# An attention forward with recurrent memory, one core: V's heads in four column tiles, V's tail rows as a pass of their own, two buffers for scaled O

## The chip, the cores and the metric

One core of a Trainium2 chip runs one program: forward and backward of a transformer block. The metric is device time in microseconds of one execution, the median over several runs. TensorE (PE) multiplies, and loads stationary operands (PEld); VectorE (DVE) and ScalarE (ACT) move results from PSUM to SBUF and do elementwise work; GpSimd (POOL) copies within SBUF and issues some DMAs; SyncE (SP) issues the others.

## The reference

Attention goes over 64 segments of 32 rows. Each segment puts 8 memory rows ahead of its own 32, attends over these 40 rows in 32 heads of 128 columns, and the first 8 rows of its output are the memory of the next segment. Around it stand a layer norm with modulation, a gated unit, and the gradients of all of it.

```python
def _A_ref(x, mem0, Wq, Wk, Wv, Wo, seg_len):
    ...
    for s in range(n_seg):
        xs = x[:, s * seg_len:(s + 1) * seg_len, :].copy()
        h = jnp.concatenate([mem, xs], axis=1)
        q = jnp.einsum('btd,dhe->bhte', h, Wq)
        k = jnp.einsum('btd,dhe->bhte', h, Wk)
        v = jnp.einsum('btd,dhe->bhte', h, Wv)
        scores = jnp.einsum('bhqe,bhke->bhqk', q, k) * scale
        scores = jnp.where(mask[None, None], scores, -1000000000.0)
        p = _softmax(scores, axis=-1)
        o = jnp.einsum('bhqk,bhke->bhqe', p, v)
        o = jnp.einsum('bhte,hed->btd', o, Wo)
        mem = o[:, :M, :].copy()
        outs.append(o[:, M:, :])
    return jnp.concatenate(outs, axis=1)

x = A_x
...
h = _layernorm(x, axis=-1) * (1 + ca) + sa
x = x + ga * _A_ref(h, A_mem0, A_Wq, A_Wk, A_Wv, A_Wo, A_seg_len)
h = _layernorm(x, axis=-1) * (1 + cb) + sb
x = x + gb * _B_ref(h, B_w_gate, B_w_up, B_w_down)
```

## The kernel before

`phase2` is the forward of the attention; the phases behind it (gated unit, its gradients, gradients of the attention, gradients of the weights) are touched only where the last segment prepares them.

A segment's 40 rows are kept as 32 rows (the memory and the first 24 of its own rows; these depend on the segment before) and 8 tail rows (its last 8; these depend on the input alone). Four segments make a tile of 128 input rows; s4 is a segment's place in its tile. The 4 x 8 tail rows of a tile (`hb`) are projected together, ahead of their segments. Heads are packed three to a group: group g holds heads 3g, 3g+1 and 3g+2 in its rows 0-31, 32-63 and 64-95, and their tail rows in 96-119. There are 11 groups of 128 columns; the last has two heads.

All projections have 32 stationary columns, so four matmuls run side by side in the four column tiles of PE, each with its own 32 rows of the PSUM tile. K and Q use all four: three for heads 0 to 23, and the fourth for heads 24 to 31.

V is computed in three chunks (`v_chunk`, line 701 on; `v_mm`, line 675) of 4, 4 and 3 groups, with one column tile for each of the three heads of a group; each goes over the four parts c of the 512 inputs. During chunks 0 and 1 the fourth column tile computes V of the tail rows of the next tile (`VTAILS`): a third of the heads per segment and the last groups in the fourth segment. `RBv` holds these rows, 32 hl + 8 s4 for head hl of a group; `v_tails` copies them with three DMAs of POOL's queue into rows 96 to 119 of the segment's `Vst`. For tile 0 `v_first` does the same work in three tiles alone.

The order is written out by hand: the program order of each engine is pinned (`self.pin(i0)`), so no engine runs anything ahead. In a segment, PE runs: K and Q (line 257), chunk 0 of V, the turns of K and Q to columns (line 880), chunk 1, the scores of 11 groups onto a mask already in PSUM (line 890), chunk 2, the sums of exponentials of thirds 0 and 1 (line 896), the products with V of thirds 0 and 1 (line 916), sums and product of third 2, a fill that depends on s4 (0: a piece of the output product of tail rows, L215; 1: the turn of a layer-normed input tile, L422; 2 and 3: the turn of projected tail rows of K or Q, L638), the turns of scaled O (line 908 for third 0, line 950 for thirds 1 and 2), small turns for the output rows of earlier segments (L339), the output product (line 223), another fill, and the sum that gives the next memory.

ACT takes the exponentials (line 892) in three thirds of 4, 4 and 3 groups into `ET`, and scales the second third of O (line 937). DVE takes the reciprocals of the sums (line 901) and scales the first and last third (line 940). `Ost` holds scaled O; it has one buffer, and its store to `OSR` in DRAM is issued by SP (line 1069) behind the stores of K and Q and the DMA transposes of V and of the probabilities. POOL normalises the transposed probabilities of the segment before (line 1118), issues `v_tails`, and copies the tail columns of K and Q of the next segment. The PSUM pool of most of this has five buffers.

The last segments also prepare the first tile of the gated unit (`first_tile_steps`): vectors are broadcast from DRAM into buffers that are no longer in use, and x1, the block's input plus the gated attention output, is formed with its statistics.

Of the kernel before, what the change touches and what calls it, by code (L numbers as in the profile page):

```python
# [40 lines left out]
class K:  # L41
# [336 lines left out]
    def phase1_setup(self, ctx, psum_tile_fn):  # L378
# [56 lines left out]
        self.xh_tile = lambda: p1w.tile([128, D], F32, name="xh", bufs=1)[:]  # L435
        self.hx_tile = lambda: p1w.tile([128, DC, 128], BF16, name="hx", bufs=3)[:]
# [10 lines left out]
    def phase2(self):  # L447
# [12 lines left out]
        self.first_x1 = wq.tile([128, D], F32, name="x1_0")  # L460
        self.first_st = wq.tile([128, 12], F32, name="st_0")
        self.glu_tiles()
        with ExitStack() as ctx:
# [31 lines left out]
            Ost = ptiles("Ost", 1)[0]  # L495
# [3 lines left out]
            RBv = ptiles("RBv", 2)  # L499
# [120 lines left out]
            def b_pieces(t):  # L620
# [30 lines left out]
                return {(3, "f1"): [P("k", 0, 4, "dve")]}, {(1, "f1"): [P("k", 4, 4, "dve")], (1, "f2"): [P("q", 0, 2, "act")],  # L651
# [13 lines left out]
            VCH = ((0, 4), (4, 4), (8, 3))  # L665

            VTAILS = {(s4, k): ((s4,) + VCH[k] + (0,),) for s4 in range(3) for k in range(2)}
            VTAILS[3, 0] = ((0, 8, 3, 0), (1, 8, 1, 3))
            VTAILS[3, 1] = ((1, 9, 2, 0), (2, 8, 2, 2))

            def v_mm(ps, j, c, lhsT, hl, a, n, o=0):

                wc = Wv[:, c, :].rearrange("p (h e) -> p h e", e=E)
                n = min(n, (H - hl + 2) // 3 - a)
# [4 lines left out]
            def v_evac(eng, dst, ps, a, n):  # L679

                m = n if a + n < G else n - 1
                self.evac(eng, dst[0:96, a * E:(a + m) * E], ps[0:96, 0:m * E])
                if m < n:
                    self.evac(eng, dst[0:64, (a + m) * E:(a + n) * E], ps[0:64, m * E:n * E])

            def hb_rows(t):
                return lambda c: hxs[t][1][:, c, :, :].rearrange("p s q -> p (s q)")

            def v_first():

                for a, n in VCH:
                    ps = psp.tile([128, 512], F32, name="pass_ps", tag="p")
                    for c in range(DC):
                        for j in range(3):
                            v_mm(ps, j, c, hb_rows(0)(c), j, a, n)
                    v_evac("dve", RBv[0], ps, a, n)
# [25 lines left out]
            def first_tile_steps():  # L722
# [6 lines left out]
                bc5 = []  # L729
# [11 lines left out]

                def bc_3():
                    bc[3] = self.xh_tile()
                    bc_load(3, bc[3])
# [10 lines left out]
                def bc_5():  # L755
                    for i in range(2):
                        bc5.append(f32(self.hx_tile().rearrange("p c x -> p (c x)")))
                        bc_load(5, bc5[i], D // 2 * i, D // 2)

                def gates():  # L760
                    for i in range(2):
                        sl = slice(D // 2 * i, D // 2 * i + D // 2)
                        nc.vector.tensor_tensor(db[:, sl], dout[:, sl], bc5[i], op=ALU.mult)
# [1723 lines left out]
```

## Time and profile before

| what | us |
|---|---|
| median of 3 runs | 2979.73 |
| their range | 2972.82 to 2981.01 |
| the profiled execution | 2976.49 |
| its span | 2974.4 |
| PE busy in it | 2905.7 |
| granted clock in it, mean | 0.997 |

The 40 slices of the span, some 74 us each; the forward takes the first 13:

```
PE   6999999999998999999999999999999999999999
PEld 3666666666665544445677777777777754445545
DVE  5565666656655788733456666666566532850011
ACT  3666666666665544312355555555555520110011
POOL 2555545545545222221344444444444432762111
PEclk9999999999999999999999999999999999999999
DMA  9898888988899998899698999999999997876565
```

A digit is the busy share of a slice in tenths. Matmuls are pipelined and each is shown with its whole latency, so a full PE may still leave gaps between starts; what PE does is read from the starts of its instructions in order of time. A line number there is that of the instruction, or of a helper that many callers share; the tile's name tells which call it is.

### The profile page before, as it was taken

To read this page: it belongs to the slowest core of one execution; us is meant where nothing else is said; L and a number is where in the kernel's file an instruction comes from. 1 tells how busy PE (TensorE), PEld (TensorE's weight loads), DVE (VectorE), ACT (ScalarE), POOL (GpSimd) and SP (SyncE) were. 2 spreads that over 40 slices of the span, in tenths; PEclk is the share of its full clock that TensorE was granted. 3 is DMA by queue.
4 is the path that set the end of the run, shared out by engine and by line. 5 is a ranking of instruction groups with operands and counts; after the bars stand their busy time and mean duration, and the time that the engine had idled before them with its cause. 6 is when DMAs were issued, how large, how long until landed. Compare 5 with 4: busy or idle time off the path is not lost.

```text
span 2974.4 us, 105326 instructions
## 1 busy us (share of the span) xinstructions
PE 2905.7 (98%) x43742; PEld 1816.9 (61%) x43816; DVE 1620.3 (54%) x3683; ACT 1348.0 (45%) x3244; POOL 1233.2 (41%) x2486
## 2 busy tenths in 40 slices
PE   6999999999998999999999999999999999999999
PEld 3666666666665544445677777777777754445545
DVE  5565666656655788733456666666566532850011
ACT  3666666666665544312355555555555520110011
POOL 2555545545545222221344444444444432762111
PEclk9999999999999999999999999999999999999999
DMA  9888898988999899998699999999999997876565
GB/s 308 221 223 220 213 218 229 217 216 224 223 226 267 209 234 229 246 280 274 190 252 256 252 250 252 249 253 247 253 251 252 247 274 246 262 252 191 161 215 171
DMA packets 838066, 703.01 MB, mean 236 GB/s; under 512 B 537698, under 2 KB 710162, under 8 KB 836692
## 3 DMA queue, kind: packets, MB, share of 16 engines
q1 hardware_dynamic: 711972, 485.29, 66.3%
q0 software_dynamic: 54512, 148.63, 15.8%
q10 hardware_dynamic: 71104, 62.34, 6.5%
q8 instruction: 345, 5.65, 0.8%
q14 instruction: 133, 1.09, 0.1%
HBM read 294.99 MB, written 276.35 MB: 192 GB/s over the span
## 4 chain that ended last, share of the span: by engine, by line
PE 89%; DMA 5%; DVE 2%; issue 2%; ACT 1%; SPq 1%; POOL 1%; DVEq 0%; POOLq 0%; ACTq 0%
PE gps L2267 14%; PE pass_ps L257 14%; PE dh_ps L215 8%; PE g_ps L1890 5%; PE pass_ps L675 5%; PE gps5o L2282 4%; PE dhq_ps L223 4%; PE at_ps L223 4%; PE mm L1371 3%; PE gps L1550 3%; PE dh_tps L215 3%; PE turn_ps L880 2%; PE mm L1331 2%; PE mm L1346 2%; PE tps L1807 2%
## 5 line engine op out<-in xcount | busy, mean ns | idle before, releaser
L2267 PE MATMUL gps<-rows,hrows 128*128 128x512 bf16 (+2 forms) x2124 | 413.6, 355 | 1.9
L2267 PEld LDWEIGHTS <-hrows 128*128 128x128 bf16 x2160 | 211.1, 98 | 204.5 <-issue 0.9
L1118 POOL TENSOR_TENSOR Pst<-Pst,rden 120x1408 bf16<-120x1408 bf16 x63 | 159.7, 2535 | 315.1 <-issue 204.0
L63 DVE CAST ot<-gps 128x512 bf16<-128x512 f32 (+3 forms) x76 | 48.2, 634 | 310.8 <-PE gps L2267 229.2
L61 ACT ACTIVATE ot<-gps 128x512 bf16<-128x512 f32 (+3 forms) x75 | 41.2, 549 | 355.0 <-PE gps L2267 228.0
L1935 POOL COPY dOst<-RAd 96x512 bf16<-96x512 bf16 x128 | 75.1, 611 | 297.0 <-DVE RAd L63 297.0
L675 PE MATMUL pass_ps<-Wv,hT 128*32 128x512 bf16 (+2 forms) x2304 | 186.7, 357 | 0.0
L2271 POOL DMA_DIRECT2D out_dram<-ot x104 | 78.5, 755 | 257.6 <-DVE ot L63 133.4
L257 PEld LDWEIGHTS <-hT 128*32 128x32 bf16 x4096 | 117.0, 97 | 96.5 <-issue 6.2
L63 DVE CAST Vst<-pass_ps 96x512 bf16<-96x512 f32 x128 | 87.1, 681 | 106.5 <-ACT RBv L61 103.0
L215 PE MATMUL dh_ps<-WvT,dVT 128*32 128x512 bf16 x2048 | 133.4, 380 | 1.8 <-DVE RBd L63 0.2
L223 PE MATMUL at_ps<-Wo,OT 128*32 128x256 bf16 x4096 | 127.8, 276 | 1.2 <-ACT OT L61 1.0
L675 PE MATMUL pass_ps<-Wv,hb 128*32 128x512 bf16 (+2 forms) x636 | 126.5, 339 | 0.2 <-POOL hb L428 0.2
L257 PE MATMUL pass_ps<-Wk,hT 128*32 128x512 bf16 x2048 | 122.7, 380 | 2.1 <-POOL hT L561 1.1
L257 PE MATMUL pass_ps<-Wq,hT 128*32 128x512 bf16 x2048 | 124.1, 381 | 0.0
L257 PE MATMUL pass_ps<-WoT,dyT 128*32 128x256 bf16 (+1 forms) x3072 | 122.6, 308 | 0.9 <-ACT dyT L2016 0.9
L223 PE MATMUL dhq_ps<-WqT,dQT 128*32 128x256 bf16 x4096 | 122.9, 273 | 0.0
L215 PE MATMUL dh_ps<-WkT,dKT 128*32 128x512 bf16 x2048 | 122.3, 380 | 0.0
L2282 PE MATMUL gps5o<-WoT,rows 128*128 128x512 bf16 x549 | 120.4, 379 | 1.2 <-DMA rows<-OSR 0.6
L223 PEld LDWEIGHTS <-dQT 128*32 128x32 bf16 x4096 | 109.8, 97 | 15.7
L317 DVE TENSOR_TENSOR dST<-dh_ps,dST 128x512 bf16<-128x512 f32 x64 | 44.3, 692 | 130.0 <-ACT dST L316 130.0
L1877 DVE SCALAR_TENSOR_TENSOR dS<-dp_ps,Pst_l 128x480 bf16<-128x480 f32 (+1 forms) x192 | 106.3, 610 | 10.0 <-PE dp_ps L1875 4.1
(475 smaller groups left out, 7038.6 us busy)
## 6 DMA issues: line engine op xcount, KB each, us to landing
OSR<-Ost SPq DMA_DIRECT2D x64, 352.0 KB
OT<-OT SPq DMA_DIRECT2D x64, 352.0 KB
PS<-Pst SPq DMA_DIRECT2D x64, 352.0 KB
Pst_l<-PS SPq DMA_DIRECT2D x64, 352.0 KB
OT_l<-OT SPq DMA_DIRECT2D x64, 352.0 KB
DVR<-rows_x POOLq DMA_DIRECT2D x64, 352.0 KB, 6.3
DKR<-rows_x POOLq DMA_DIRECT2D x64, 352.0 KB, 6.1
DQR<-rows_x POOLq DMA_DIRECT2D x64, 352.0 KB, 3.2
```

Of the source, the lines that this page charges most:

```text
L63: return nc.vector.tensor_copy(out, in_)
L215: self.nc.tensor.matmul(ps[32 * j:32 * j + 32, :], lhsT=lhsT, rhs=w, start=(n < 4), stop=(n >= total - 4), tile_position=(0, 32 * j))
L223: nc.tensor.matmul(ps[32 * j:32 * j + 32, :], lhsT=x[k], rhs=w[k][:, 256 * d:256 * d + 256], start=(n == 0), stop=(n == total - 1), tile_p ...
L257: self.nc.tensor.matmul(ps[32 * j:32 * j + 32, :], lhsT=lhs(c), rhs=rhs, start=(c == 0), stop=(c == DC - 1), tile_position=(0, 32 * j))
L675: nc.tensor.matmul(ps[32 * j:32 * j + 32, o * E:(o + n) * E], lhsT=lhsT, rhs=wc[:, 3 * a + hl:3 * (a + n - 1) + hl + 1:3, :], start=(c == ...
L1118: nc.gpsimd.tensor_tensor(Pst[0:120, :, :], Pst[0:120, :, :], rden[:, :].unsqueeze(2).to_broadcast([120, G, 128]), op=ALU.mult)
L1371: nc.tensor.matmul(hp[:], lhsT=xT[:, fc, :], rhs=wT[:, fc, :], start=(n == 0), stop=(n == 2 * FC - 1))
L1550: nc.tensor.matmul(ps[:], lhsT=h2r[:, j, c * 128:(c + 1) * 128], rhs=xr[:, j, :], start=(j == 0), stop=(j == NT - 1))
L1877: nc.vector.scalar_tensor_tensor(out=part3(dS, pi)[:, :, 0:120], in0=ps[:, 0:n, 0:120], scalar=cfg.scale, in1=part3(Pst, pi)[:, :, 0:120], ...
L1890: nc.tensor.matmul(ps[:, j, 0:w], lhsT=lh[:, g * GW:(g + 1) * GW], rhs=rh[:, g * GW:g * GW + w], start=True, stop=True)
L2267: nc.tensor.matmul(ps[:, 0:ng * E], lhsT=hrows[:, tp_, c * 128:(c + 1) * 128], rhs=rows[:, tp_, 0:ng * E], start=(tp_ == 0), stop=(tp_ == ...
L2282: nc.tensor.matmul(pss[gg][:], lhsT=rows[:, t, gg * E:(gg + 1) * E], rhs=dyrows[:, t, :], start=(n == 0), stop=(n == NTP - 1))
```

## The change

V's heads are dealt out as K's and Q's are. The chunks have 3, 3 and 2 groups in the first three column tiles, which makes 8 groups; the fourth column tile computes the remaining groups 8 to 10: those of the first head in chunk 0 (three groups), of the second in chunk 1 (three), of the third in chunk 2 (two). DVE evacuates all chunks' 96 rows and the fourth tile's rows of chunks 0 and 1, and ACT the fourth tile's rows of chunk 2.

V of the tail rows becomes `v_tail`: a pass over two steps of 128 columns in four column tiles, four such passes per tile, evacuated by DVE, one in each segment, at a new place "gap" between the turns of O's first third and those of the others. For tile 0 two passes of four steps take the place of `v_first`. `RBv` now has the form of K's and Q's tail rows, and `v_tails` copies it with six DMAs instead of three.

`Ost` has two buffers, and 120 of its 128 rows are stored. The fill that followed the product of O's last third is issued ahead of that third's sums and product.

x1 of the first tile lies in the memory of Wk instead of a tile of its own, so its last step comes behind K's last pass; two broadcast vectors are loaded in halves into other buffers; and the input buffers of the gated unit's tiles are dealt out in another order.

```diff
-            Ost = ptiles("Ost", 1)[0]
+            Osts = ptiles("Ost", 2)
...
-            RBv = ptiles("RBv", 2)
+            RBv = ptiles("RBv", 2, w=9 * 128)
...
-                return {(3, "f1"): [P("k", 0, 4, "dve")]}, {(1, "f1"): [P("k", 4, 4, "dve")], (1, "f2"): [P("q", 0, 2, "act")],
+                V = lambda u: (lambda: v_tail(t, u, 2, "dve"))
+                return {(3, "f1"): [P("k", 0, 4, "dve")], (3, "gap"): [V(0)]}, {
+                        (0, "gap"): [V(2)], (1, "gap"): [V(4)], (2, "gap"): [V(6)], (1, "f1"): [P("k", 4, 4, "dve")], (1, "f2"): [P("q", 0, 2, "act")],
...
-            VCH = ((0, 4), (4, 4), (8, 3))
-
-            VTAILS = {(s4, k): ((s4,) + VCH[k] + (0,),) for s4 in range(3) for k in range(2)}
-            VTAILS[3, 0] = ((0, 8, 3, 0), (1, 8, 1, 3))
-            VTAILS[3, 1] = ((1, 9, 2, 0), (2, 8, 2, 2))
+            VCH = ((0, 3), (3, 3), (6, 2))
...
+            def v_tail(t, u, n, eng):
+
+                runs = [(hl, max(u, 3 * hl), min(u + n, 3 * hl + 3)) for hl in range(3)]
+                ps = psp.tile([128, 512], F32, name="pass_ps", tag="p")
+                for c in range(DC):
+                    hb = hxs[t][1][:, c, :, :].rearrange("p s q -> p (s q)")
+                    for j in range(3):
+                        v_mm(ps, j, c, hb, j, u, n)
+                    for hl, a, b in runs:
+                        if a < b:
+                            v_mm(ps, 3, c, hb, hl, 8 + a - 3 * hl, b - a, a - u)
+                self.evac(eng, RBv[t % 2][:, u * E:(u + n) * E], ps[:, 0:n * E])
...
             def v_chunk(s, k):
 
-                t, s4 = s // nseg_t, s % nseg_t
                 a, n = VCH[k]
-                tails_of = VTAILS.get((s4, k), ()) if t + 1 < NT else ()
+                m = 3 if k < 2 else 2
                 ps = psp.tile([128, 512], F32, name="pass_ps", tag="p")
                 hT = get_ht(s)
                 for c in range(DC):
                     for j in range(3):
                         v_mm(ps, j, c, hT[:, c, :], j, a, n)
-                    for of in tails_of:
-                        v_mm(ps, 3, c, hb_rows(t + 1)(c), *of)
-                if k > 0:
-                    v_evac(("dve", "act")[k - 1], Vsts[s % 2], ps, a, n)
-                for hl, ta, tn, o in tails_of:
-                    self.evac(("act", "dve")[k], RBv[(t + 1) % 2][32 * hl:32 * hl + 32, ta * E:(ta + tn) * E],
-                              ps[96:128, o * E:(o + tn) * E])
-                if k == 0:
-                    v_evac("dve", Vsts[s % 2], ps, a, n)
+                    v_mm(ps, 3, c, hT[:, c, :], k, 8, m)
+                Vst = Vsts[s % 2]
+                self.evac("dve", Vst[0:96, a * E:(a + n) * E], ps[0:96, 0:n * E])
+                self.evac(("dve", "dve", "act")[k], Vst[32 * k:32 * k + 32, 8 * E:(8 + m) * E], ps[96:128, 0:m * E])
...
                 for j in range(3):
-                    nc.gpsimd.dma_start(Vst[96 + 8 * j:104 + 8 * j, :], rb[32 * j + o:32 * j + o + 8, :])
+                    nc.gpsimd.dma_start(Vst[96 + 8 * j:104 + 8 * j, 0:8 * E], rb[32 * j + o:32 * j + o + 8, 0:8 * E])
+                    nc.gpsimd.dma_start(Vst[96 + 8 * j:104 + 8 * j, 8 * E:11 * E], rb[96 + o:104 + o, 3 * E * j:3 * E * (j + 1)])
...
+                    first_tile[3]()
                     nc.gpsimd.dma_start(self.w_gate, io["B_w_gate"].rearrange("(c p) f -> p c f", p=128))
...
-                    v_first()
+                    for u in (0, 4):
+                        v_tail(0, u, 4, "dve")
...
                 ost(1, or1, "act")
+                fill(s4, "turn")
+                if s == 2 or s4 == 1 and s > 1:
+                    p1(s // nseg_t + P1_AHEAD, 4, evacs)
+                if s4 == 0:
+                    tail.chunk()
                 den(2, or2)
                 early = s4 == 1 and len(self.later) > 1
                 pv(2, or2)
                 recip(2, 3, or2)
                 ost(2, or2, "dve")
-                fill(s4, "turn")
-                if s == 2 or s4 == 1 and s > 1:
-                    p1(s // nseg_t + P1_AHEAD, 4, evacs)
                 if s == NS - 1:
                     turn_v(2)
-                if s4 == 0:
-                    tail.chunk()
                 ott_first()
+                fill(s4, "gap")
                 if early:
                     self.pop_later()
                 ott_rest()
...
-                nc.sync.dma_start(self.OSR[s], gl3(Ost))
+                nc.sync.dma_start(self.OSR[s, 0:120], gl3(Ost)[0:120])
...
-        self.ring_dout += [self.flat(Wk, 2 * n + i * D, D) for i in range(4)]
+        self.ring_dout += [self.flat(Wq, 2 * n, D)] + [self.flat(Wk, 2 * n + i * D, D) for i in range(4)]
+        self.first_x1 = self.flat(Wk, 2 * n + 2 * D, 2 * D, F32)
```

More of the change, by code (lines that the diff above doesn't have):

```diff
@@ L435, in phase1_setup @@
         self.xh_tile = lambda: p1w.tile([128, D], F32, name="xh", bufs=1)[:]
+        self.x0_tile = lambda: p1w.tile([128, D], BF16, name="x0_1", bufs=1)[:]
+        self.h1_tile = lambda: p1w.tile([128, D], BF16, name="h1", bufs=1)[:]
         self.hx_tile = lambda: p1w.tile([128, DC, 128], BF16, name="hx", bufs=3)[:]
@@ L740, in bc_4, with bc_halves @@
                     bc_load(4, bc[4])
+                def bc_halves(i, tiles):
+                    bcs = bc[i] = []
+                    for k, t in enumerate(tiles):
+                        bcs.append(f32(t))
+                        bc_load(i, bcs[k], D // 2 * k, D // 2)
                 def bc_3():
-                    bc[3] = self.xh_tile()
-                    bc_load(3, bc[3])
+                    bc_halves(3, (self.x0_tile(), self.h1_tile()))
                 def x_rows():
@@ L755, in bc_5 @@
                 def bc_5():
-                    for i in range(2):
-                        bc5.append(f32(self.hx_tile().rearrange("p c x -> p (c x)")))
-                        bc_load(5, bc5[i], D // 2 * i, D // 2)
+                    bc_halves(5, [self.hx_tile().rearrange("p c x -> p (c x)") for _ in range(2)])
                 def gates():
@@ L853, in phase2 @@
                     slots[0, "f1"] = first_piece[3, "f1"]
+                    pieces[0, "gap"] = first_piece[3, "gap"] + pieces[0, "gap"]
                 if s4 == 0:
@@ L860, in phase2 @@
                 hT_next = get_ht(s + 1) if s + 1 < NS else None
-                QT, KT, Vst, ET, OT = XT["q"], XT["k"], Vsts[s % 2], ETs[s % 2], OTs[s % 2]
+                QT, KT, Vst, ET, Ost, OT = XT["q"], XT["k"], Vsts[s % 2], ETs[s % 2], Osts[s % 2], OTs[s % 2]
                 RA = RAs[s % 2]
```

40 lines of the change are left out of this document (12 added, 28 removed).

## The prediction

> **What bounds the kernel now.** I read the page first, then the forward's waits, then two segments instruction by instruction. The page says that TensorE never rests:
>
> ```profile
> span 2974.4 us, 105326 instructions
> ...
> PE 2905.7 (98%) x43742; PEld 1816.9 (61%) x43816; DVE 1620.3 (54%) x3683; ACT 1348.0 (45%) x3244; POOL 1233.2 (41%) x2486
> ...
> PE 89%; DMA 5%; DVE 2%; issue 2%; ACT 1%; SPq 1%; POOL 1%; DVEq 0%; POOLq 0%; ACTq 0%
> ```
>
> The change touches the forward alone: 64 segments, from 40 to 945 us. Busy time by stretch (columns: us, then PE, PEld, DVE, ACT, POOL, clock, DMA share, GB/s) over two of its segments shows the period, 14.0 us, a full PE at full clock, and room on DVE, ACT and POOL:
>
> ```profile
> 500.12:514.10 13.98, 13.98 (x278) 8.72 (x274) 8.03 (x19) 9.30 (x24) 6.97 (x14) 1.00 0.90 222
> 514.10:528.11 14.01, 13.85 (x289) 9.21 (x285) 7.95 (x19) 9.57 (x25) 6.69 (x14) 1.00 0.96 220
> ```
>
> So the price of the change is read from starts on PE (start, duration, what, count), here in segment 33, which has s4 = 1:
>
> ```profile
> 513.11 0.40 PE L675 MATMUL pass_ps<-Wv,hT 128*32 128x512 bf16 x3
> ...
> 514.10 0.62 PE L880 MATMUL turn_ps<-ident,RA1k 128*128 128x128 bf16 x8
> ...
> 515.09 0.40 PE L675 MATMUL pass_ps<-Wv,hT 128*32 128x512 bf16 x3
> ...
> 516.07 0.75 PE L890 MATMUL st_ps<-qT,kT 128*128 128x120 bf16 x11
> 516.75 0.83 PE L675 MATMUL pass_ps<-Wv,hT 128*32 128x384 bf16 x12
> 517.51 0.37 PE L896 MATMUL or_ps<-ones,ET 128*128 128x1 bf16 x8
> ...
> 519.03 0.39 PE L908 MATMUL tps<-ident,Ost 120*128 120x120 bf16 x4 [0.16 <-DVE Ost L940]
> ```
>
> A chunk of V (513.11, 515.09, 516.75) runs until the next line's start: 0.985, 0.98 and 0.76 us. Four steps over c and one change of tile shape make it up, and the widest matmul of a step sets the step: at 512 columns 0.216 us, at 384 0.163, at 256 0.11 (the output product's 16 steps, 506.06 to 507.89, give 0.114); the change is the rest, some 0.11. The fourth tile rides free beside the other three.
>
> **Heads in four tiles.** Chunks 0 and 1 go from 512 to 384 columns: 4 x 0.053 = 0.21 us less each. Both lie ahead of the scores and nothing there is near: ScalarE no longer evacuates RBv first, so kT is ready no later, and qT (VectorE, two evacuations of 384 by 0.56, between the rows of 0.43 at 256 and 0.69 at 512, then 0.87 for the turns) ends some 0.1 us before its last third is read. I take -0.43 per segment.
>
> Chunk 2 goes from 384 to 256: 0.21 us less on its own. I give it nothing. Its cover is the exponentials: the first sums of the scores read ET, and
>
> ```profile
> 516.54 1.03 ACT L892 ACTIVATE ET<-st_ps 128x480 bf16<-128x480 f32 x2 [0.48 <-ACT kT L61]
> ```
>
> shows the second third of ET ready at 517.57. Four of the eight sums at 517.51 need it, so they cannot end before 517.57 + 0.05 + 4 x 0.025 = 517.72, which is when they end now. A shorter chunk 2 starts the sums at 517.30 and lets PE stand for 0.2 us.
>
> **Its evacuation moves from ACT to DVE**, ahead of the reciprocal on which all of O hangs. By 128x256 out of PSUM at 0.425 us (L232) it runs from 517.44 to 517.86; the reciprocal starts at 517.99 now. Free, with 0.12 us to spare.
>
> **Tail rows as a pass.** Per tile four passes of 256 columns, one per segment, between the turns of O: 4 x 0.11 = 0.44, plus two changes of tile shape. A chunk of the tail product has both in this trace (s4 = 0):
>
> ```profile
> 504.35 0.33 PE L916 MATMUL or_ps<-Vst,ET 128*128 128x128 bf16 x3
> 504.61 0.62 PE L215 MATMUL ao_tps<-Wo,ao_tail 128*32 128x512 bf16 x8
> 505.16 0.39 PE L908 MATMUL tps<-ident,Ost 120*128 120x120 bf16 x4
> 505.38 0.69 PE L950 MATMUL tps<-ident,Ost 120*128 120x120 bf16 x7
> 505.91 0.22 PE L339 MATMUL at_tp<-ident,at_tb 128*128 128x128 bf16 x1
> ```
>
> Three matmuls at 0.055 would let the next start at 504.52; it starts at 504.61. Two steps of 0.216 would end at 505.04; the turns start at 505.16, less their own 0.02 of latency. So 0.19 for both, and 0.63 per pass. Before, this work was free in the fourth tile.
>
> The pass fills waits. Seven turns at 0.053 take 0.37, and 505.38 to 505.91 is 0.53: 0.16 of waiting for O. By the same reading: 0.12 with s4 = 1 (before the turns at 519.58), 0.25 with 2, 0.27 with 3. Moving the turn of a projection or the tail chunk ahead of the third part of O delays that part's scaling by the fill (0.2 to 0.6 us), and the pass hides this; the first turns still wait for O's first part at 519.03. With s4 = 0 the fill covers 0.07 that den now waits for the reciprocal. Four segments cost 4 x 0.63 - 0.16 - 0.12 - 0.25 - 0.27 - 0.07 = 1.65 and give 8 x 0.216 = 1.73: **-0.1 per four segments.**
>
> Against this stand two waits that no row prices. The pass takes one more of five PSUM buffers; with s4 = 2, where two small turns follow, the output product would get the one that the pass leaves, 0.15 us late (DVE then evacuates O's third part, the turns 0.40 and the pass 0.43 in that order). And PE's first product with V waits for six DMAs where it was three, each pair of waits about 0.05. Bounds: 0 and 0.25 per four segments. I take the middle: with the -0.1 it is **0 over segments 1 to 58**, give or take 2 us.
>
> **Two buffers for O.** VectorE waited for the store of the last O (waits of the forward: us in total, times, longest):
>
> ```profile
> PE tps L908 <- DVE Ost L940: 7.8, 22, 1.1
> ...
> DVE Ost L940 <- DMA OSR<-Ost: 4.0, 5, 1.3
> ```
>
> Five times, and each shows in the period (segment 24: the turns start 1.1 us late). At least 0 (if SyncE, which issues the store of O 6 to 12 us after the reciprocal, stalls another buffer), at most the 7.8 that PE stood there. I take **-4**.
>
> **The rest.** Segments 59 to 63 have no pass: the 0.43 of chunks 0 and 1 is kept, about 0.2 of it lost again because O's third part is scaled later: **-1**. Segment 0's V runs before Wq lands at 40.47 (the chain waits 27 us for that DMA): nothing. POOL issues six DMAs per segment for three, 3 x 0.53 = 1.6 us; behind them stand kT's and qT's tail copies, read 8 us later, and POOL sits idle for 4 us before each norm. Without that cover kT would be late by 1.6. SP gets no more DMAs; the store of O loses 8 of 128 rows. x1's add goes behind the last K pass; it and its statistics have a whole segment. The loads in halves and one more copy at the end are off PE's path.
>
> Sum: 0 - 4 - 1 = **-5 us**. Against the profiled execution's 2976.5 that is 2971.5; the runs' median is 3.2 above that execution, 2974.7. I say **2973**.
>
> **Rivals.**
> *VectorE becomes the limit (slower).* It gets four evacuations of 0.56 and two of 0.425 where it had two of 0.68 and one of 0.69: 1.0 us more per segment (8.0 to 9.0 of 14), all of it between the scores and the scaling of O. If it is still at chunk 1's columns at 517.44, chunk 2's evacuation pushes the reciprocal, and O with it, by up to 0.42. It decides from 0.12 us of delay on. At half of it, 0.2 x 62 segments = +12: 2984; for it, two narrow evacuations cost nearly as much each as one wide; against it, my sum leaves 0.12.
> The Trainium skill's TensorEngine Tiling (Array Packing), section PSUM Bottleneck, warns of this: tiling speeds up TensorE but not the evacuation, and both ScalarE and VectorE should be used. The trace agrees that rows don't count: 32x512 takes VectorE 0.693 and 96x512 0.681.
> *The pass gets O's own buffer (slower).* If its PSUM buffer is that of the third part of O, it waits for that part's scaling, about 0.55: x 57 = +31, 3004. Against it: by then the buffer of the first part is free.
> *The saving of chunk 2 is kept (faster).* If the exponentials follow the scores sooner: 0.2 x 62 = -12 more, 2961. Against it: ACT is idle for 0.48 before them already and waits for the scores' own matmuls.
> *O's buffer is worth more (faster).* The runs lie 8 us apart; if that is the store of O, two buffers bring -10 to -12: 2965.
> *It does not pay at all:* another buffer stalls in O's place, -1: 2976, no change.
>
> **Chances.** Under 0.3% (8.9 us) a measurement of this kernel cannot tell. The forecast with "no pay" 0.50; chunk 2 kept 0.10; O worth more 0.22; VectorE 0.14; the buffer 0.04. The two that are faster cross the bound: 0.32; the two slower 0.18. The range takes in all but the ends, 2962 to 2984; the forecast's own is 2969 to 2978.
>
> **What would show it.** Chunks 0 and 1 at 0.77 us each; the sums of the scores in two groups, four and four, 0.2 us apart; the reciprocal no later after the scores than 1.92 us; a pass of 0.63 between the turns with no wait behind it; no wait of Ost for OSR; segments of 13.9 to 14.1 us. The forecast is wrong if the reciprocal comes later, if the pass itself waits, or if the period moves by over 0.15 us.

## The result and the profile after

The changed kernel takes 2983.70 us (median of 11 runs, 2978.67 to 2986.59), the kernel before 2977.87 (11 runs, 2972.82 to 2981.01): ratio 1.0020, interval 1.0010 to 1.0029. It is 5.8 us slower, where 5 us faster was forecast. The profiled execution is the changed kernel's quickest, 2978.67, so its trace shows 2.5 of the 5.8 us. Its page:

```profile
span 2976.9 us, 108128 instructions
...
PE 2907.1 (98%) x44934; PEld 1832.1 (62%) x45008; DVE 1690.0 (57%) x3860; ACT 1308.9 (44%) x3105; POOL 1338.8 (45%) x2679
...
PE 88%; issue 2%; DVE 2%; DMA 2%; ACT 1%; POOL 1%; SPq 0%; DVEq 0%; POOLq 0%; ACTq 0%
```

On this page nothing looks worse: DMA's share of the chain falls from 5% to 2%. Segment 33 on PE (start, duration, what, count) is as forecast too:

```profile
512.94 0.84 PE L673 MATMUL pass_ps<-Wv,hT 128*32 128x384 bf16 x16
513.71 0.62 PE L874 MATMUL turn_ps<-ident,RA1k 128*128 128x128 bf16 x8
...
518.46 0.39 PE L902 MATMUL tps<-ident,Ost 120*128 120x120 bf16 x4 [0.22 <-DVE Ost L934]
518.78 0.62 PE L673 MATMUL pass_ps<-Wv,hb 128*32 128x256 bf16 x16
519.33 0.26 PE L327 MATMUL ao_b_ft<-foldsel,ao_b_hi 128*128 128x32 bf16 x4
```

Chunk 0 runs 0.77 us to the next start, the tail pass 0.55. Four undisturbed segments take 56.01 us from scores to scores, 55.95 before. What changed is where PE waits between 62 and 938 us (us in total, times, longest):

```profile
PE tps L902 <- DVE Ost L934: 3.9, 17, 0.3
PE mod_ps L200 <- DMA wmod_r<-in_w_mod_dram: 3.7, 5, 1.0
PE at_ft L242 <- ACT at_hi L230: 3.4, 5, 1.3
```

No wait of Ost for OSR is left (the 3.9 are 17 times 0.2, part of the period). But PE now waits five times for a piece of w_mod that comes late (before: twice, 1.2 us), and longer for ACT's `at_hi` (before: 1.9 us in 4). Three of these waits, 0.5 us each in segments 59, 61 and 62, stand in both traces; the other two, 2.0 us in segments 2 and 14, have s4 = 2, where `at_hi` stands on ACT behind the copy of turned K tails, which waits for GpSimd to have read the old ones. And in segment 63 GpSimd works off a late norm ahead of the power that x1's scale needs:

```profile
940.08 2.53 POOL L1113 TENSOR_TENSOR Pst<-Pst,rden 120x1408 bf16<-120x1408 bf16 x1 [2.78 <-issue]
942.58 0.57 POOL L764 TENSOR_TENSOR st<-st 128x1 f32<-128x1 f32 x1
```

```profile
943.19 0.55 DVE L767 TENSOR_SCALAR RBv<-Wk,st 128x512 f32<-128x512 f32 x1 [2.83 <-POOL st L764]
```

Before, the same norm began at 934.84, 3.4 us ahead of segment 63's scores; now it begins 1.3 us behind them. DVE, and with it the reciprocal, stands for 2.83 us.

The two traces side by side, by the starts of the scores on PE (us):

| stretch | before | after | difference |
|---|---|---|---|
| up to segment 0 | 45.25 | 44.71 | -0.5 |
| segments 0 to 4 | 75.50 | 75.26 | -0.2 |
| 5 to 58: period | 13.5 x 55.95 | 13.5 x 56.01 | +0.8 |
| 5 to 58: above it, scores to output product | 3.86 | 0.33 | -3.5 |
| 5 to 58: above it, output product to next scores | 1.78 | 7.04 | +5.3 |
| 59 to 62 | 56.44 | 55.17 | -1.3 |
| 63, scores to output product | 4.22 | 7.89 | +3.7 |
| the rest | 2031.95 | 2030.23 | -1.7 |

The "above it" rows are the sums, over the 54 segments, of what each lasted beyond the ordinary length of its kind (the third shortest with the same s4). Of the 7.04 us, 4.2 lie in segments with s4 = 3, where w_mod's piece is late, and 2.8 in those with s4 = 2, where `at_hi` is.

### The profile page after: what moved, and what is told of

Same layout as the page of the kernel before. It is cut to its first block, busy times and chain, and to the rows that moved or that the text cites. A ratio compares the mean times of both kernels' runs of the same rounds, so it can differ in the third digit from the quotient of the medians.

```text
span 2976.9 us, 108128 instructions
## 1 busy us (share of the span) xinstructions
PE 2907.1 (98%) x44934; PEld 1832.1 (62%) x45008; DVE 1690.0 (57%) x3860; ACT 1308.9 (44%) x3105; POOL 1338.8 (45%) x2679
## 3 DMA queue, kind: packets, MB, share of 16 engines
q0 software_dynamic: 60656, 148.65, 15.8%
## 4 chain that ended last, share of the span: by engine, by line
PE 88%; issue 2%; DVE 2%; DMA 2%; ACT 1%; POOL 1%; SPq 0%; DVEq 0%; POOLq 0%; ACTq 0%
PE gps L2262 14%; PE pass_ps L257 13%; PE dh_ps L215 8%; PE g_ps L1885 5%; PE pass_ps L673 4%; PE gps5o L2277 4%; PE dhq_ps L223 4%; PE mm L1366 3%; PE at_ps L223 3%; PE dh_tps L215 3%; PE gps L1545 3%; PE turn_ps L874 2%; PE mm L1326 2%; PE mm L1341 2%; PE tps L1802 2%
## 5 line engine op out<-in xcount | busy, mean ns | idle before, releaser
L63 DVE CAST Vst<-pass_ps 96x384 bf16<-96x384 f32 (+2 forms) x320 | 168.6, 527 | 57.5 <-PE pass_ps L673 51.2
L673 PE MATMUL pass_ps<-Wv,hT 128*32 128x384 bf16 (+1 forms) x3072 | 146.8, 310 | 0.0
L223 PEld LDWEIGHTS <-OT 128*32 128x32 bf16 x4096 | 100.0, 96 | 17.4 <-ACT OT L61 6.1
```

What stands on the lines that cost most here:

```text
L63: return nc.vector.tensor_copy(out, in_)
L223: nc.tensor.matmul(ps[32 * j:32 * j + 32, :], lhsT=x[k], rhs=w[k][:, 256 * d:256 * d + 256], start=(n == 0), stop=(n == total - 1), tile_p ...
L673: nc.tensor.matmul(ps[32 * j:32 * j + 32, o * E:(o + n) * E], lhsT=lhsT, rhs=wc[:, 3 * a + hl:3 * (a + n - 1) + hl + 1:3, :], start=(c == ...
```

## The experiments

All were timed in five rounds beside the kernel before; ratios are to it.

### One part alone

```diff
-            Osts = ptiles("Ost", 2)
+            Osts = ptiles("Ost", 1) * 2
```

> The changed kernel with one buffer for scaled O instead of two; V's order, the tail pass and all moves stay. It is the V part by itself. The forecast's sum (V 0, second buffer -4): 4 us slower than the changed kernel, about 2988, with Ost waiting for OSR again in segments such as 1, 9, 24 and 43, 0.5 to 1.1 us each. Theory 'brake' (without that wait the SP queue's stores run later against PE, so the piece of w_mod lands late and the norm of segment 62 too): the waits of mod_ps for wmod_r fall from 3.7 us to about 1.2, the norm of segment 62 starts ahead of segment 63's scores as before, and what the wait of Ost costs is given back there: the time stays at 2982 to 2985.

Measured: 2990.8 us, 1.0050 (1.0033 to 1.0068). In its waits between 62 and 938 us:

```profile
PE tps L902 <- DVE Ost L934: 21.3, 31, 2.6
...
DVE Ost L934 <- DMA OSR<-Ost: 18.8, 17, 2.5
```

The kernel before had 4.0 us in 5 waits of DVE. The waits for wmod_r did fall, to 0.2 us, as "brake" had it, but the norm of segment 62 began 2.5 us behind the next scores and not ahead of them, and the time rose by 7 us over the changed kernel, more than either theory allowed. **With the V part (the six DMAs and the moves for x1 are in it) the store of O comes later**, and the second buffer hides some of it.

The other part alone: V's code and order as before, and the second buffer with the moves that make room for it (the lines of the diff that show it, against the changed kernel):

```diff
-            VCH = ((0, 3), (3, 3), (6, 2))
+            VCH = ((0, 4), (4, 4), (8, 3))
...
-            RBv = ptiles("RBv", 2, w=9 * 128)
+            RBv = ptiles("RBv", 2)
```

> The kernel before with the second buffer for scaled O and what makes room for it (x1 in spare columns of Wk, x1's add behind the last K pass, the modulation rows in halves, the store of 120 rows), but with V's chunks, tails and order as before. The forecast's term: the waits of Ost for OSR are gone and the time is 4 us below the kernel before, about 2974. Theory 'brake': the waits are gone, and what they cost comes back as waits of mod_ps for wmod_r and as a late norm in segment 63, so the time is 2977 to 2979. Theory 'last tile': segment 63 loses 2 to 3 us as in the changed kernel, because x1's add and statistics are late here too; the time is about 2976.

Measured: 2984.6 us, 1.0024 (1.0012 to 1.0035). Slower, against all three. Its profiled run is its quickest, 2974.87, and shows no wait for OSR, 3.3 us of `mod_ps` for wmod_r and 5.88 us in segment 63: the "brake" is in it, but not the 10 us by which the median lies above it. Above the period, scores to output product, this trace shows 0.35 us for 3.86 before, and output product to next scores 3.73 for 1.78.

### The places where it shows

Each of the three places was mended by itself: the norm of segment 62 behind the power; w_mod's load ahead of the segment's stores; GpSimd's tail copies ahead of the six DMAs.

```diff
                 if s == NS - 1:
                     first_tile[4]()
+                    norms.pop()()
```

> The changed kernel with one move in the last segment: GpSimd's scaling of Pst of segment 62 (the norm) is issued behind the power of x1's statistics and not ahead of it. Theory 'last tile' (the loss sits in segment 63, where the first tile's scale on VectorE waited 2.83 us for the power, which stood behind the norm on GpSimd): the scale follows its statistics at once, the reciprocal of segment 63 and the two products behind it come some 3 us earlier, from scores to output product in segment 63 goes from 7.89 us to about 5, the span falls by about 3 us and the time from 2983.7 to about 2981. Rival 'the ring is late' (the norm is late because the SP queue is, and the last segment only shows it): the norm, its store and the last PS stores end later by as much, the time stays within 1 us of 2983.7.

Measured: 2984.1 us (1.0009 to 1.0036). Segment 63 fell from 7.89 to 5.69 us as the first theory had it; the time did not: segment 55 alone lost 4.4 us in this trace, 2.6 of it to wmod_r.

```diff
-                    load()
                     mod_r.append(products)
...
+                if s + 1 in mod_at and s + 1 != 4:
+                    early_mod.append(self.mod_rest(psp, sb2, mod_at.index(s + 1)))
+                    early_mod[0][0]()
                 if s < NS - 1 and norms:
```

> The changed kernel with the load of the next piece of w_mod issued at the start of a segment, ahead of that segment's stores on SP, instead of behind the store of OT (15 of the 16 pieces; the one for segment 4 stays). Theory: the waits of mod_ps for wmod_r (3.7 us in 5 segments) are gone and the time falls by 3 to 4 us, to about 2980. Rival (PE is held elsewhere in these segments and the wait only covers it, or the stores behind the load come later by as much): within 1 us of 2983.7.

Measured: 2978.69 us, 1.0008 (1.0000 to 1.0017), a gain of 5 by the medians (the changed kernel's interval, 1.0010 to 1.0029, overlaps). The waits for wmod_r are gone, but those for `at_hi` grew from 3.4 to 9.0 us in the profiled run. What the gain comes from its trace does not show.

```diff
-                    v_tails(s + 1)
                     if s4 < 3:
                         tails_in("kq", s + 1)
+                    v_tails(s + 1)
```

> The changed kernel with two steps of GpSimd exchanged in every segment: the copies of K's and Q's tail columns for the next segment ahead of the six DMAs of V's tail rows, instead of behind them. Theory 'GpSimd's queue' (the six DMAs, 0.54 us each, hold up the last reader of the buffer b_cols, so in the segments with s4 = 2 ACT's copy of turned K tails waits for it, the high half of the output product behind it on ACT is late, and PE waits at at_ft: 2.8 us over segments 6, 10, 14, 46, 50 and 54 of the profiled run): these waits fall under 1 us in all, and the time from 2983.7 to about 2981. Rival (V's tail rows, now later, are the next thing to be late: the transposing load of VTr waits for them on the SP queue, and everything behind it there comes later): no gain, 2983 to 2986, with more waits of mod_ps for wmod_r.

Measured: 2986.34 us (1.0017 to 1.0038). The rival: `at_hi` 1.0 us instead of 3.4, and `mod_ps` 14.5 instead of 3.7.

All three, with w_mod loaded a segment sooner and not ahead of the stores:

```diff
-                if s + 1 in mod_at:
+                for at in (s + 1, s + 2):
+                    if at in mod_at and (at == 4) == (at == s + 1):
```

> The changed kernel with three moves together: GpSimd's scaling of Pst of segment 62 behind the power of x1's statistics; K's and Q's tail copies ahead of V's tail rows; each piece of w_mod loaded one segment sooner, at the same place among the stores (15 of 16). If the three are separate causes and each gives what its own wait shows (2.2 us in segment 63, 2.8 us of b_cols, 3.7 us of wmod_r), the time is 2983.7 - 8.7, about 2975, at or below the kernel before. If one ring is late and these waits are only where it shows, the waits move on, to the reads of RA by the stores of KST and QST or to segment 63, and the time is 2979 to 2983.

Measured: 2978.03 us, 1.0004 (0.9995 to 1.0013). The time lies between the two forecasts, and the waits moved on: PE stood 5.6 us for the next product until DVE had copied `RBq`. Mending one place shifts the wait to the next, which speaks for something late behind all of them.

### The six DMAs

The kernel before, its three copies of V's tail rows split in six:

```diff
-                    nc.gpsimd.dma_start(Vst[96 + 8 * j:104 + 8 * j, :], rb[32 * j + o:32 * j + o + 8, :])
+                    nc.gpsimd.dma_start(Vst[96 + 8 * j:104 + 8 * j, 0:8 * E], rb[32 * j + o:32 * j + o + 8, 0:8 * E])
+                    nc.gpsimd.dma_start(Vst[96 + 8 * j:104 + 8 * j, 8 * E:11 * E], rb[32 * j + o:32 * j + o + 8, 8 * E:11 * E])
```

> The kernel before with nothing changed but the copies of V's tail rows: six DMAs of 8 heads and of 3 heads in place of three of 11 heads. Theory 'six DMAs' (they are what makes GpSimd and the DMA ring later in the changed kernel; with one buffer of scaled O that comes out as waits for OSR, as in the run with one buffer): the waits of Ost for OSR grow from 3.9 us over segments 5 to 58 towards 13.7, and the time rises by 6 to 12 us over the kernel before, to 2983 to 2989. Rival (the forecast: the three added DMAs are hidden; the waits of the run with one buffer come from V's part being later on VectorE or from the pass): within 2 us of the kernel before.

Measured: 2989.3 us, 1.0036 (1.0022 to 1.0049). By the medians this edit alone costs more than the whole change (12.5 us against 5.8; the intervals overlap). The bytes are the same, 16 and 6 KB in two DMAs for 22 KB in one; what is added is 96 packets a segment. The profiled run is its longest, 2995.65; the waits in it, and last the same wait in the kernel before:

```profile
ACT b_colsk L61 <- POOL kT L65: 15.9, 12, 2.2
...
PE tps L909 <- DVE Ost L941: 10.4, 15, 1.6
DVE Ost L941 <- DMA OSR<-Ost: 10.3, 12, 1.4
```

```profile
ACT b_colsk L61 <- POOL kT L65: 1.8, 3, 0.9
```

Two things hold PE for most of the 22 us above the period. The store of O is late (8.4 us above the period between scores and output product). And 10.1 us lie between output product and next scores in segments with s4 = 2, where ACT's copy of the turned K tails waits for GpSimd's copies behind the six DMAs, and `at_hi` and PE wait behind it.

Is it GpSimd's time or the transfers? The same time on GpSimd without a transfer:

```diff
+                for j in range(3):
+                    nc.gpsimd.tensor_copy(idle[0:96, :], idle[0:96, :])
```

> The kernel before with three copies of a small tile onto itself on GpSimd (96 x 400, some 0.55 us each) behind the three DMAs of V's tail rows in every segment: GpSimd is as busy as with six DMAs, and no packet is added. Theory 'GpSimd's queue' (the price of the six DMAs, 12.5 us in the run with six, is the time that they take on GpSimd, which the norm and the tail copies behind them pay): 2985 to 2990, with waits of Ost for OSR of 8 us or more. Rival 'packets' (it is the added transfers in the DMA queues that delay the others): within 2 us of the kernel before.

Measured: 2974.59 us, 0.9995 (0.9985 to 1.0004). **The added time on GpSimd costs nothing by itself.** But in its trace the norm begins 3.0 us ahead of the next scores on average (segments 2 to 61), against 0.3 us before and 0.3 us behind them with six DMAs, with 1.0 us above the period instead of 5.6. Why it got ahead stays open, and so does what the same copies would cost behind a late norm, where the trace with six DMAs shows GpSimd's tail copies holding up ACT.

The changed kernel with three DMAs, the fourth column tile's heads copied to their rows on ACT, then on DVE:

```diff
-                self.evac(eng, RBv[t % 2][:, u * E:(u + n) * E], ps[:, 0:n * E])
+                self.evac(eng, rb[0:96, u * E:(u + n) * E], ps[0:96, 0:n * E])
+                for hl, a, b in runs:
+                    if a < b:
+                        o = (8 + a - 3 * hl) * E
+                        self.evac("act", rb[32 * hl:32 * hl + 32, o:o + (b - a) * E], ps[96:128, (a - u) * E:(b - u) * E])
```

> The changed kernel with V's tail rows in three DMAs again: RBv is 11 heads wide, and each part of the tail pass copies its fourth column tile to the rows of its heads by one or two short copies on ACT. Theory 'six DMAs': GpSimd's norm starts 0.4 us or more earlier against PE, the waits of b_cols and of wmod_r shrink from 7 us to 3 or less, the time falls from 2983.7 to about 2979. Rival: within 1.5 us of the changed kernel, and then the ring's lateness is that of the second buffer alone.

Measured: 3002.3 us (1.0063 to 1.0091). The copy stands on ACT ahead of OT's, and PE waits for OT (13.8 us in 29 segments): a segment takes 14.45 us. But 0.5 us is all that lies above that period, and the norm runs 2.6 us ahead of the scores.

> The changed kernel with V's tail rows in three DMAs and the short copies of the fourth column tile on VectorE (in the run before they were on ACT, ahead of OT's copies, and PE waited there for OT 0.4 us in every segment). Theory 'six DMAs': the steady period goes back to the changed kernel's 56.0 us for four segments, GpSimd's norm starts earlier than in the changed kernel (mean 0.37 us behind the next scores), the excess over the steady period in segments 5 to 58 falls from 7.4 us to under 4, and the time is 2978 to 2981. Rival 'the ring has a period of its own of about 14 us' (the run before was free of its waits only because PE was slower, 14.44 us a segment): at 14.0 us the waits of b_cols and wmod_r are back, and the time is 2982 to 2985.

Measured: 2983.3 us (1.0009 to 1.0030), the rival's time. Above the period there are 3.2 us instead of 7.4, but the copies still hold PE (9.9 us for `RBv`), so the two DMA layouts are not compared cleanly here.

The moves again, on this kernel and on the second buffer alone:

> The kernel of the run above with the norm of segment 62 behind the power, each piece of w_mod one segment sooner, and the last segment's third tail copy of V on VectorE instead of ACT, where it stood ahead of the exponentials. If the causes add up: segment 63 from scores to output product 4.5 us instead of 7.89, no wait of mod_ps, the time 2971 to 2974, below the kernel before. Rival (V's part gains nothing and the ring takes back the rest): 2976 to 2979.

> The kernel with the second buffer for scaled O alone (V as in the kernel before, three DMAs as there), with two of the moves: the norm of segment 62 behind the power, each piece of w_mod one segment sooner. Theory: its loss against the kernel before (+7.8 us) is the late pieces of w_mod and the last segment, so both gone it shows the forecast's gain of the second buffer, 2972 to 2974. Rival 'brake' (without the wait of Ost the ring runs as late as it can and finds another place): 2977 to 2982.

Measured: 2980.6 (1.0003 to 1.0021) and 2980.0 us (1.0001 to 1.0022): the first above its rival's range, the second in it. In the first, segment 63 still takes 7.43 us; in the second it is back at 4.22, and there are 8.0 us above the period elsewhere.

### The ring

What the late stores, loads and norms share is SyncE's queue. In the kernel before, segment 36 to 37 (SyncE's issues, then GpSimd):

```profile
566.22 2.58 SPq L1040 DMA_TRANSPOSE Pst<-ET  x1
...
570.31 0.32 SPq L1120 DMA_DIRECT2D VT<-VTr  x1
574.28 0.32 SPq L1121 DMA_DIRECT2D PS<-Pst  x1
574.70 1.49 SPq L606 DMA_DIRECT2D KST<-RA1k  x1
```

```profile
571.72 2.54 POOL L1118 TENSOR_TENSOR Pst<-Pst,rden 120x1408 bf16<-120x1408 bf16 x1 [4.74 <-issue]
```

The transposing load of Pst goes out at 566.22; the norm begins at 571.72, after it has landed; its end at 574.26 releases the store of PS, for which SyncE has stood since 570.63; and behind it the next stores of K and Q and the next two transposing loads wait their turn. That is a closed loop, once per segment. Its steps, as means over the segments 6 to 58 whose norm began at most 1 us ahead of the scores (37 before, 44 changed, 46 with six DMAs):

| step | before | changed | before, six DMAs |
|---|---|---|---|
| issue of Pst to norm | 4.99 | 5.03 | 5.37 |
| norm to store of PS | 3.14 | 3.27 | 3.20 |
| to KST | 0.45 | 0.49 | 0.54 |
| to VTr's issue | 3.43 | 3.30 | 3.41 |
| to Pst's issue | 1.88 | 1.94 | 1.87 |
| loop | 13.90 | 14.03 | 14.38 |
| PE's own period | 13.99 | 14.00 | 13.99 |

Where a loop is closed its length equals the segment's by necessity; what tells that it sets the pace is that little else is waited for in it. SyncE's issues from PS to the next Pst follow each other with 0.1 us between them, 0.2 to 0.4 ahead of VTr's; and PS goes out at the norm's end in 22 of the 37 segments before (24 of 44, 28 of 46), while in the others SyncE, whose issues alone take 11.1 us of a segment, comes to it later. The steps vary with the issues' own lengths (0.38 to 1.49 us for a store of K), for which no run here shows the reason.

So the loop is as long as PE's period: it is a second bound, met with nothing to spare. In the long run with six DMAs it is longer than PE's 13.99, and the segments 5 to 58 do take 14.40 us each, the loop's 14.38. That the six DMAs are what lengthens it there is less sure: the changed kernel has them too, and its step from Pst to norm is 5.03, near the 4.99 before.

The cut: GpSimd stores PS itself, behind its norm.

```diff
-                    nc.sync.dma_start(self.PS[s], Pst[:])
+                    nc.gpsimd.dma_start(self.PS[s], Pst[:])
```

> The kernel before with one change: the store of PS is issued by GpSimd, right behind its norm, and not by SP, which waits for the norm there with all of the next segment's stores and transposing loads behind it. Theory 'ring' (SP's queue, Pst's transposing load, norm and PS's store are a loop of about 14 us, as long as PE's period): without that wait the stores run ahead of PE; KST goes out at 1.5 us or less behind the scores instead of 3.5, the waits of Ost for OSR and of wmod_r (5.6 us over segments 5 to 58) fall under 1 us, the time from 2977.7 to 2971 to 2974. Rival 'packets' (the transfers are late because the DMA engines are full, 0.89 of their time): the waits stay, the time within 2 us of the kernel before.

Measured, on the kernel before: 2971.19 us, 0.9975 (0.9965 to 0.9985). The longest wait for OSR that is left:

```profile
DVE Ost L940 <- DMA OSR<-Ost: 1.1, 1, 1.1
```

None for wmod_r; 0.8 us above the period; KST goes out 1.6 us ahead of the scores instead of 3.5 behind. A change of one line that beats both kernels, with one buffer for O. It does two things at once, and no run separates them: SyncE no longer waits for the norm, and 352 KB a segment leave its queue (161.9 MB on it before, 142.5 now, between 120 and 900 us).

> The kernel before with six DMAs for V's tail rows (2989.3 us) and the store of PS issued by GpSimd. Theory 'ring': the six DMAs cost by making the loop longer than PE's period (14.4 us a segment); with the loop cut they cost no more than 2 us over the run of the kernel before with the same cut, 2972 to 2976. Rival 'packets' (the added transfers slow all others, whatever the queue's order): 2984 to 2989 still.

Measured: 2974.52 us, 0.9987 (0.9978 to 0.9996). The six DMAs cost 12.5 us with the loop and 3.3 without it (2974.52 against 2971.19; these two intervals overlap). That is the ring's forecast, and the rival's 2984 to 2989 is out.

> The changed kernel with the store of PS issued by GpSimd. Theory 'ring': the excess over the steady period falls from 7.4 us to under 2, the norm of segment 62 is done ahead of the power of x1's statistics, so segment 63 takes 5 to 6 us from scores to output product instead of 7.89; the time falls by 8 to 10 us to 2974 to 2976. Rival 'packets' or 'last tile alone': 2980 to 2984.

Measured: 2978.44 us, 1.0000 (0.9989 to 1.0011): 5 us better than the changed kernel, above the ring theory's 2974 to 2976 and short of the rival's 2980 to 2984. 4.7 us above the period remain, 3.2 of them in segments 34 and 38, where PE waits for `at_hi`. GpSimd, with the six DMAs and now the store of PS, still holds up ACT's copy there; in this trace the norm is late again up to segment 36.

> The changed kernel with the store of PS issued by GpSimd, the norm of segment 62 behind the power of x1's statistics, and the last segment's third tail copy of V on VectorE. Theory 'ring': segment 63 at 4.5 us from scores to output product, no waits left in segments 5 to 58, the time 2971 to 2974, below the kernel before by the forecast's 5 us. Rival: the moves in segment 63 give nothing more than the cut alone, 2974 to 2976.

Measured: 2974.68 us, 0.9989 (0.9980 to 0.9998), in the rival's range; 3.2 us above the period remain. Segment 63 takes 5.61 us: x1's scale no longer waits for the power, but it stands behind four evacuations of V on DVE, and the reciprocal starts 3.31 us behind the scores there where it was 1.91 before the change.

> The kernel with the second buffer for scaled O alone (V as in the kernel before), with the store of PS issued by GpSimd. Theory 'ring': its loss against the kernel before (7.8 us) goes with the cut; what is left over the kernel before with the cut (2971.2) is the 1.7 us of segment 63, where x1's scale is late: 2972 to 2974. The forecast's -4 for the buffer would show as 2967 to 2968; a loss that has nothing to do with the ring as 2977 or more.

> The changed kernel with one buffer for scaled O (the V part alone), with the store of PS issued by GpSimd. Theory 'ring': the waits of Ost for OSR (13.7 us over segments 5 to 58 in the run with one buffer) fall under 2 us and the time from 2990.8 to 2976 to 2979, the same as with two buffers (2978.4). Rival (the V part itself makes Ost wait): 2984 or more.

Measured: 2971.0 us, 0.9985 (0.9976 to 0.9994), and 2974.9 us, 0.9996 (0.9988 to 1.0005), each some 1 us below the ring theory's range. The four corners, ratios to the kernel before in thousandths (the two lines in the middle have the moves for x1 in them as well):

| | PS stored by SyncE | by GpSimd |
|---|---|---|
| V as before, one Ost | 0 | -2.5 (-3.5 to -1.5) |
| second Ost alone | +2.4 (+1.2 to +3.5) | -1.5 (-2.4 to -0.6) |
| V part alone | +5.0 (+3.3 to +6.8) | -0.4 (-1.2 to +0.5) |
| both: the change | +2.0 (+1.0 to +2.9) | 0.0 (-1.1 to +1.1) |

With the loop, the V part costs 5 without the second buffer, the second buffer costs 2.4 without the V part, and on top of the V part it gains 3. So what one part is worth depends on the other. Cut, the second buffer makes no difference that the intervals can tell (-2.5 and -1.5; -0.4 and 0.0), and the V part keeps a price of some 2, about 6 us, 3.3 of which the six DMAs would make up.

**The loop does not account for the whole loss.** The cut helps both kernels alike: with it the changed kernel takes 7.3 us more than the kernel before (2978.44 against 2971.19, intervals apart), without it 5.8.

## Why the prediction was wrong

**V's heads in four tiles: right.** Chunks of 0.77 us; chunk 2 gives nothing (segment 33: sums 1.33 us and product 1.66 us behind the scores, 1.44 and 1.67 before); the reciprocal 1.90 us behind the scores where at most 1.92 was asked for. The 0.12 of spare time on DVE is used up: the last evacuation ends at 517.41 and the reciprocal starts at 517.41. So the rival of VectorE as the limit did not come, but nothing is left to spare; that its 2984 is the measured time is luck. The pass did not wait for O's buffer, and chunk 2's saving was not kept.

**The tail pass: right in sum, in part by luck.** +0.06 us per four segments where 0 was said. But a pass takes 0.55 us where 0.63 was summed (the two changes of tile shape some 0.11 and not 0.19; for the 0.02 of latency in that term no row stands), and scores to output product still grew by 1.72 per four segments where 1.65 was said: some 0.4 of the waits that the pass was to fill stayed.

**Two buffers for O: the step failed.** Its waits went, 3.5 us in the trace, inside "0 to 7.8". But "-4" took a wait's end for a gain. OSR was late because SyncE's queue was, and PE's wait for it was one of the places where that queue held PE back. With that hold gone PE is held elsewhere: +5.3 us in the changed kernel, +2.0 with the buffer alone. Alone, the buffer makes the kernel 7.8 us slower by the medians; with the loop cut there is no such loss. The rival that "does not pay at all: another buffer stalls in O's place" named this mechanism; it put it at -1.

**"POOL issues six DMAs per segment for three ... behind them stand kT's and qT's tail copies, read 8 us later": the second failure, in two ways.** The sum took the 1.6 us on GpSimd as covered by its 4 us of idle time before each norm. That holds while the norm is early, as in the run with copies in the DMAs' place, which cost nothing. Behind a late norm it fails: kT's tail copies then come late, and they have a second reader of their time, for with s4 = 2 ACT waits for the buffer that they free, and PE behind it (2.8 us above the period in the changed kernel, 10.1 in the long run with six DMAs).

What the three DMAs added besides was not asked for: 96 packets a segment (54512 to 60656 on that queue in all) on DMA engines that are busy for 0.89 of the time between 120 and 900 us. In the long run with six DMAs the norm begins 0.38 us later after the issue of Pst, and the loop exceeds PE's period; in the changed kernel's trace this step is 0.04 longer. "SP gets no more DMAs" was true and no answer: the loop can grow without one. The Trainium skill's DMA: Bandwidth & Descriptors, section Issuing engines are not separate DMA queues, says that DMAs of all engines run on the same 16 DMA engines and interleave. The longer step in the long run fits this, but no run here separates the packets from GpSimd's time behind a late norm, nor shows through which of the 16 engines' queues a delay would pass.

**"x1's add goes behind the last K pass; it and its statistics have a whole segment": the third.** The power of these statistics stands on GpSimd behind the norm, and the norm hangs on the loop; +3.7 us in the profiled run. With the norm moved 2.2 of them went, with the cut alone 1.8, and with the cut, the norm and one evacuation moved 2.3. What is left there stands in V's evacuations, ahead of x1's scale on DVE.

The undisturbed period was forecast within 0.02 us a segment. What failed was to sum up PE alone, where a second loop had the same length; the profile before showed it, in SyncE's wait for the norm (us in total, times, longest):

```profile
SPq L1121 <- POOL Pst L1118: 82.9, 33, 2.7
```

What stays open: the profiled runs show 2.5 of the 5.8 us, and in the run with the second buffer alone none of the 7.8; neither trace is of one of the longer runs. That each part alone loses through the loop is borne out by the cut, measured against the kernel before with the same cut: from 2.4 to 1.0 thousandths for the buffer, from 5.0 to 2.1 for the V part. For the change as a whole it is not (2.0 and 2.5). So the loop shows why the 4 us of the buffer did not come, and not all of why the change is slower. Of the 7.3 us with the cut, 3.3 would be the six DMAs, and 1.8 stand in segment 63 (6.06 us against 4.22); for the rest no run here shows the cause.

## What to carry to other kernels

Before a wait is removed, ask what made the awaited thing late, and follow the waits of the queues (store, norm, load) until they close into a loop; if its length per turn is that of the busiest engine, a sum over that engine alone is not a forecast, and small additions to the loop can cost more than they look. Then try to cut the loop first. Here the store that waited for a computation did better in the queue of the engine that computes, by 6.7 us, than at the head of the queue that feeds everybody.

## What was not expected of the hardware

Splitting three DMAs of 22 KB a segment into six of 16 and 6 KB cost 12.5 us over 64 segments, and 3.3 with the loop cut; 1.6 us of copies a segment on the engine that issues them cost nothing, with the norm 3 us ahead. In the kernel before the norm's start wanders from 3.4 us ahead of the scores to 2.6 us behind them over some 60 segments. Where PE was slowed to 14.45 us it stayed ahead from segment 14 on, and in the kernel before with the loop cut from segment 5 on, by 2.6 and 3.8 us in the mean of segments 2 to 61. In the changed kernel with the cut it was still behind at segment 36. The spread of the runs does not follow this simply: with the cut it fell for the second buffer alone (17.5 us to 12.4) and rose for the changed kernel (7.9 to 16.6).
